# A decode kernel's gate moved ahead of six query rounds, its down product moved to TensorE, two transfers cut in halves

## The chip, the cores and the metric

The kernel runs on one core of a Trainium2 chip. The metric is device time in microseconds (us). Of the kernel before, three runs took 696.61, 697.62 and 699.97 us; the median is 697.62. One more execution was recorded by the hardware profiler.

The engines have short names in the profile: PE is TensorE (PEld its weight loads), DVE is VectorE, ACT is ScalarE, POOL is GpSimd, SP is SyncE, which issues nearly all transfers here. "Queue" means SP's transfer queue. A "handover" is one engine's wait for another's semaphore.

## The reference

One token of a decoder block. `x` is one row of 512, normed to `xn`. Attention has 32 heads of 128 against cached keys and values of 8192 positions; a gated unit of 1376 columns gives a row of 512, whose silu scales the attention's output.

```
xn = layernorm(x)
q  = (xn @ wq).reshape(32 heads, 128)
p  = softmax(q . k_cache * 128**-0.5)          # 8192 positions a head
s  = (p @ v_cache).reshape(4096) @ wo          # 4096 -> 512
h  = sigmoid(xn @ w_gate) * (xn @ w_up)        # 1376
g  = silu(h @ w_down)                          # 512
out = x + s * g
```

All in float32. Keys and values are 134 MB each, so 268 of the 294 MB that the kernel reads.

## The kernel before, in words

Heads are taken in 16 pairs. The keys of a pair are one transfer of 8.39 MB into a slot of 128 partitions by 16384 numbers (64 partitions a head, 128 positions on each); its values are another. SBUF has room for three such slots, A, B and C. The keys of pairs 0, 2, 4, ... go to B and those of odd pairs to A; the values of all pairs but the last go to C, those of the last to B. K0 is the keys of pair 0, V0 its values, and so on.

**Transfers.** SP issues them in program order, and each waits until its slot is free: `wq` into C, the three weights of the gated unit into A, K0 into B (L144 to L151). Then K1 into A, once the gate is done (L322, L323: a wait on `n_gate`, the count after the matmuls of L258). Then V0 into C, once all eight rounds of queries have read `wq` (L332: a wait on `s_q`), and from there by turns K(n+2), which waits for VectorE to be done with the keys of pair n (`k_free`, L338), and V(n+1), which waits for PE to be done with the values of pair n (`s_po`, L335). At the end come V15 into B (L341) and `wo` into C in five pieces (L344).

**Queries** (L210 to L222). A round t makes 512 columns of `xn @ wq`, four heads, with four matmuls into PSUM bank t. The moving operand is `wq`, the stationary one is `xn` spread over 128 columns (`xnb`). ACT copies each round into `q_all`. Rounds 0 to 3 run first (L226), rounds 4 to 7 behind the turned products of the gated unit (L241).

**Gated unit.** VectorE makes the weighted sums of `w_gate` and `w_up` over four blocks of rows (L198, L201), and PE sums these over the partitions and turns them, 11 matmuls of one column each (L235, L236), into banks 0 and 1. Sigmoid (L240) and a product (L244) give `hid`. VectorE then multiplies the ten full blocks of `w_down` by their columns of `hid` and adds them up (L247: L198, L201) and the last block of 96 rows (L250). PE sums over the partitions with four matmuls (L258), ACT takes the sigmoid (L262), and VectorE multiplies it by its argument after the scores of pair 0 (L330).

**A pair.** VectorE multiplies the keys by the query and sums over 128 numbers, in two halves (L277, L279: four passes), then takes the maximum (L282), which PE turns and spreads (L304, L306). ACT takes the exponentials into `prz` (L293). PE adds up the row sums (L308), multiplies `prz` with the values in 32 matmuls in four column groups (L313), and picks the heads' rows (L318). On PE pairs 0 to 14 are a loop (L347), pair 15 stands behind it (L349).

**End.** The heads are divided by their sums and turned (L356 to L364), multiplied by `wo` (L374, L378: a wait for each piece), scaled by the gate, and added to `x` (L391, L393).

Each engine follows its own program in order; nothing reorders it.

Of the kernel before, what the change touches and what calls it, by code (L numbers as in the profile page):

```python
# [25 lines left out]
def kernel(  # L26
# [17 lines left out]
    NP = H // 2  # L44
# [62 lines left out]
    po, pt, pm, g_ps, acc, fold_ps, o_ps, oTl = bank  # L107

# [7 lines left out]
    names = "x xr wg wu wd wr wq k0 k1 va".split()  # L116
# [34 lines left out]
    d["k0"].by(sp.dma_start(B, rows_of(k_src, 0)), 16)  # L151
# [12 lines left out]
    dve.memset(rs2, 0.0)  # L164
    dve.wait_ge(s_pool.sem, 2)
# [60 lines left out]
    queries(0, nq // 2)  # L226
# [3 lines left out]
    for a, (name, t) in enumerate((("wg", wg_t), ("wu", wu_t))):  # L230
# [7 lines left out]
        if a == 0:  # L238
            act.wait_ge(s_pe.sem, n)
            n_sg = s_act.by(act.activation(sg, turned[0], AF.Sigmoid))  # L240
    queries(nq // 2, nq)  # L241
    dve.wait_ge(s_act.sem, n_sg)
    dve.wait_ge(s_pe.sem, n)
    s_dve.by(dve.tensor_mul(hid, sg, turned[1]))  # L244
    self_wait()
    dve.wait_ge(d["wd"].sem, 16)
    weighted(wd_t[:, 0, :], lambda r: wd_t[:, r, :], lambda r: hid[:, r:r + 1], FP)  # L247
    self_wait()
    dve.wait_ge(d["wr"].sem, 16)
    s_dve.by(dve.scalar_tensor_tensor(wd_t[:FL, 0, :], wd_rest[:FL, :], hid[:FL, FP:FP + 1], wd_t[:FL, 0, :],  # L250
                                      op0=ALU.mult, op1=ALU.add))
    n_wr = s_dve.n
    pool.wait_ge(s_dve.sem, n_wr)
    n_prz = s_pool.by(pool.memset(prz.rearrange("p j a -> p (j a)"), 0.0))
    act.wait_ge(s_pool.sem, n_prz)
    pe.wait_ge(s_dve.sem, n_wr)
    for g in range(NG):
        m = pe.matmul(g_ps[g * GP:g * GP + 1, :GC], ones[:, 0:1], wd_t[:, 0, g * GC:(g + 1) * GC],  # L258
                      start=True, stop=True)
# [9 lines left out]
    def scores(n):  # L269
        kt = k_slot(n).rearrange("p (j d) -> p j d", d=Dh)  # L270
        s = sc[n % 2]
        h = NB // 2
        q = q_all[:, n:n + 1, :].to_broadcast([P, h, Dh])
        dve.wait_ge(k_sem(n).sem, 16 * (n // 2 + 1))
        for i in range(2):
            part = kt[:, i * h:(i + 1) * h, :]
            s_dve.by(dve.tensor_mul(part, part, q))  # L277
# [24 lines left out]
    def pair(v, landed):  # L302
# [3 lines left out]
        pe.matmul(pm[:, 0:2], ones[:1, :], mx[:1, 2:4], start=True, stop=True).then_inc(s_pm, 1)  # L306
        take(pe, s_pr)
        pe.matmul(oTl[:, 2:4], ones, rs2, start=True, stop=True)  # L308
        nj = NB // ROWS
        landed()  # L310
        for j in range(nj):
            g = j % NG
            m = pe.matmul(po[g * GP:g * GP + 2 * ROWS, :], prz[:, j * ROWS:(j + 1) * ROWS, :],  # L313
                          v[:, j * QT:(j + 1) * QT], start=(j < NG), stop=(j >= nj - NG))
# [26 lines left out]
    d["va"].by(sp.dma_start(B, rows_of(v_src, NP - 1)), 16)  # L341
# [87 lines left out]
```

## Time and profile before

| | |
|---|---|
| profiled execution, its own time | 697.02 us |
| its span in the trace | 695.1 us |
| DVE busy | 587.8 us (85%) |
| PE busy | 241.8 us (35%) |
| ACT busy | 41.4 us (6%) |
| SP's queue | 97.8% of 16 engines' span |
| read from HBM | 293.67 MB |
| mean TensorE clock granted | 0.651 |

Rows of groups read: line, engine, operation, out<-in, shapes, count, then busy time and idle time ahead of it. Rows in order of time read: start, duration, engine, line, operation, and in brackets the idle time before it with what ended it. Rows by stretch read: stretch, its length, then PE, PEld, DVE, ACT and POOL busy time (with counts of instructions), granted TensorE clock, DMA share, GB/s. One float32 matmul is two instructions in these rows.

### The profile page before, as it was taken

What the parts mean: (1) busy time and instruction counts of PE and PEld (TensorE: products, weight loads), DVE (VectorE), ACT (ScalarE), POOL (GpSimd) and SP (SyncE); (2) the same over time, 40 slices, a digit from 0 to 9 for tenths busy, and PEclk for the clock granted to TensorE, in tenths of its full rate; (3) what the DMA queues carried; (4) which work ended last, traced back from release to release, by engine and by line L of the source; (5) the groups of instructions that cost most, each with busy time, mean ns of one, the idle gap of its engine ahead of it and who ended that gap; (6) DMA issues with size and microseconds to landing.
All of it is one profiled execution on the core that took longest, in us unless ns stands there. A gap on an engine that the chain in (4) does not pass through costs nothing. (4 is left out here: it accounts for less than half of the span.)

```text
span 695.1 us, 3534 instructions
## 1 busy us (share of the span) xinstructions
PE 241.8 (35%) x1490; PEld 91.0 (13%) x1490; DVE 587.8 (85%) x140; ACT 41.4 (6%) x135; POOL 1.0 (0%) x7
## 2 busy tenths in 40 slices
PE   0499005123060505043140506051230605050367
PEld 0274001101010101001010101011010101010022
DVE  0348999999989989798979989798979899798950
ACT  0021010101010000001010000001010100000010
POOL 0000000000000000000000000000000000000000
PEclk9988556657565757556575756565575656575579
DMA  9994999999999999999999999999999999999997
GB/s 392 402 465 192 420 422 422 426 457 441 427 422 426 434 456 434 422 426 426 460 437 422 426 422 464 437 422 426 422 464 434 426 426 422 464 434 426 426 420 307
DMA packets 6181, 293.74 MB, mean 423 GB/s; under 512 B 824, under 2 KB 832, under 8 KB 1184
## 3 DMA queue, kind: packets, MB, share of 16 engines
q1 hardware_dynamic: 5912, 293.47, 97.8%
q10 hardware_dynamic: 264, 0.20, 0.1%
q8 instruction: 3, 0.05, 0.0%
q14 instruction: 2, 0.02, 0.0%
HBM read 293.67 MB, written 0.00 MB: 422 GB/s over the span
## 5 line engine op out<-in xcount | busy, mean ns | idle before, releaser
L277 DVE TENSOR_TENSOR slot<-slot,q_all 128x8192 f32<-128x8192 f32 x32 | 277.9, 8684 | 31.2 <-DMA slot<-in_A_k_cache_dram 31.2
L279 DVE TENSOR_REDUCE sc<-slot 128x64 f32<-128x8192 f32 x32 | 277.9, 8686 | 1.1
L313 PE MATMUL psum<-slot,prz 128*8 128x512 f32 x1024 | 146.9, 738 | 272.2 <-PEq L130 272.2
L313 PEld LDWEIGHTS psum<-slot,prz 128*8 128x8 f32 x1024 | 30.1, 103 | 375.5 <-issue 375.4
L304 PE MATMUL psum<-ident,mx 128*1 128x128 f32 x32 | 9.4, 395 | 107.3 <-PEq L130 107.3
L297 ACT COPY o<-psum 128x512 f32<-128x512 f32 x16 | 9.4, 585 | 431.5 <-PE psum L313 431.5
L213 PE MATMUL psum<-slot,o 128*128 x64 | 32.7, 676 | 1.6 <-DVE o L204 1.6
L318 PE MATMUL psum<-pick,o 128*128 128x2 f32 x128 | 16.4, 250 | 12.8 <-PEq L130 12.8
L318 PEld LDWEIGHTS psum<-pick,o 128*128 128x128 f32 x128 | 15.5, 191 | 27.2 <-issue 27.2
L308 PE MATMUL psum<-rs,ones 128*128 128x2 f32 x32 | 8.9, 349 | 23.4 <-PEq L130 23.4
L179 DVE TENSOR_REDUCE st<-x_col 128x1 f32<-128x4 f32 x1 | 0.2, 157 | 19.9 <-DMA x_col<-in_A_x_dram 19.9
L213 PEld LDWEIGHTS psum<-slot,o 128*128 128x128 f32 x64 | 13.8, 220 | 19.0 <-issue 19.0
L304 PEld LDWEIGHTS psum<-ident,mx 128*1 128x1 f32 x32 | 1.8, 80 | 108.4 <-issue 108.4
L284 DVE TENSOR_REDUCE mx<-psum 1x2 f32<-1x128 f32 x16 | 4.5, 279 | 12.3 <-PE psum L304 12.3
L293 ACT ACTIVATE prz<-sc,mx 64x128 f32<-64x128 f32 x32 | 13.0, 405 | 0.7
L356 DVE RECIPROCAL heads<-heads 128x32 f32<-128x32 f32 x1 | 0.4, 354 | 13.4 <-ACT heads L299 13.4
L306 PE MATMUL psum<-mx,ones 1*128 1x2 f32 x32 | 8.9, 344 | 7.4 <-PEq L130 7.4
L308 PEld LDWEIGHTS psum<-rs,ones 128*128 128x128 f32 x32 | 8.0, 312 | 24.3 <-issue 24.3
L289 ACT ACTIVATE mx<-psum 128x2 f32<-128x2 f32 x16 | 2.8, 172 | 129.8 <-PE psum L306 129.8
L201 DVE SCALAR_TENSOR_TENSOR slot<-slot,xn 128x1376 f32<-128x1376 f32 x6 | 9.9, 1652 | 0.2
L306 PEld LDWEIGHTS psum<-mx,ones 1*128 1x128 f32 x32 | 8.0, 307 | 14.9 <-issue 14.9
L175 PE MATMUL psum<-st,ones 128*128 128x1 f32 x4 | 1.2, 362 | 24.8 <-DVE st L179 23.9
(57 smaller groups left out, 72.5 us busy)
## 6 DMA issues: line engine op xcount, KB each, us to landing
slot<-in_A_wo_dram SPq DMA_DIRECT2D x1, 4096.0 KB, 19.1
slot<-in_B_w_gate_dram SPq DMA_DIRECT2D x1, 2752.0 KB, 28.2
slot<-in_B_w_up_dram SPq DMA_DIRECT2D x1, 2752.0 KB, 34.2
slot<-in_B_w_down_dram SPq DMA_DIRECT2D x1, 2560.0 KB, 39.7
slot<-in_A_wo_dram SPq DMA_DIRECT2D x1, 2048.0 KB, 23.5
slot<-in_A_wo_dram SPq DMA_DIRECT2D x1, 1280.0 KB, 26.1
slot<-in_A_wo_dram SPq DMA_DIRECT2D x1, 512.0 KB, 26.9
slot<-in_A_k_cache_dram SPq DMA_DIRECT2D x16, 42.4
```

The costliest lines, as they stand in the source:

```text
L201: s_dve.by(dve.scalar_tensor_tensor(acc, t(k), col(k), acc, op0=ALU.mult, op1=ALU.add))
L213: m = pe.matmul(psum[:, bass.ds(t * QT, QT)], xnb[:, k, :], wq_t[:, k, bass.ds(t * QT, QT)], start=(k == 0), stop=(k == KT - 1))
L277: s_dve.by(dve.tensor_mul(part, part, q))
L279: s_dve.by(dve.reduce_sum(s[:, i * h:(i + 1) * h], part, axis=AX.X))
L284: dve.reduce_max(mx[:1, 2:4], pt[:1, :P].rearrange("p (a m) -> p a m", a=2), axis=AX.X).then_inc(s_am, 1)
L293: e = act.activation(prz[r, :, a], sc[n % 2][r, :], AF.Exp, bias=mx[r, 4 + a:5 + a], scale=SCALE, accum_out=rs2[r, a:a + 1])
L297: act.copy(o1, po).then_inc(s_o1, 1)
L304: pe.matmul(pt[:1, :P], mx[:, 0:1], ident, start=True, stop=True).then_inc(s_pt, 1)
L306: pe.matmul(pm[:, 0:2], ones[:1, :], mx[:1, 2:4], start=True, stop=True).then_inc(s_pm, 1)
L308: pe.matmul(oTl[:, 2:4], ones, rs2, start=True, stop=True)
L313: m = pe.matmul(po[g * GP:g * GP + 2 * ROWS, :], prz[:, j * ROWS:(j + 1) * ROWS, :], v[:, j * QT:(j + 1) * QT], start=(j < NG), stop=(j >= ...
L318: m = pe.matmul(oTl[:, 0:2], o1[:, b * Dh:(b + 1) * Dh], pick[:, 2 * b:2 * b + 2], start=(b == 0), stop=(b == ROWS - 1))
```

## The change

It has four parts. Line numbers behind the first part are 1 to 16 higher in the changed kernel.

1. Only query rounds 0 and 1 run ahead of the gated unit. Rounds 2 to 7 follow once the gate's row is finished (`n_grow`). The down product is no longer VectorE's: PE takes `hid` as stationary column and the blocks of `w_down` as moving operand, in four column groups of one bank (`gate_ps`), VectorE copies the bank (`gsum`), and four matmuls with `sel`, a column of ones at the four groups' rows, add the groups up. Sigmoid and product follow at once. VectorE clears the two banks at the program's start. The clearing of `prz` moves from GpSimd to VectorE.
2. K0 comes in two transfers of half the columns each, and the scores of pair 0 begin on the first half.
3. V15 comes in two such transfers, and its product begins on the first half.
4. In pair 15 PE runs four matmuls of 512 columns into `g_ps`, whose result nobody reads: three ahead of the maximum, one ahead of the row sums.

```diff
-    queries(0, nq // 2)
+    queries(0, 2)
...
-    queries(nq // 2, nq)
     dve.wait_ge(s_act.sem, n_sg)
     dve.wait_ge(s_pe.sem, n)
-    s_dve.by(dve.tensor_mul(hid, sg, turned[1]))
-    self_wait()
-    dve.wait_ge(d["wd"].sem, 16)
-    weighted(wd_t[:, 0, :], lambda r: wd_t[:, r, :], lambda r: hid[:, r:r + 1], FP)
...
+    n_hid = s_dve.by(dve.tensor_mul(hid, sg, turned[1]))
+    pe.wait_ge(s_dve.sem, n_hid)
+    pe.wait_ge(d["wd"].sem, 16)
+    for r in range(FP):
+        g = r % NG
+        m = pe.matmul(gate_ps[g * GP:g * GP + 1, :], hid[:, r:r + 1], wd_t[:, r, :], start=(r < NG), stop=(r >= FP - NG + 1))
+    pe.wait_ge(d["wr"].sem, 16)
+    g = FP % NG
+    m = pe.matmul(gate_ps[g * GP:g * GP + 1, :], hid[:FL, FP:FP + 1], wd_rest[:FL, :], start=False, stop=True)
+    n_gate = s_pe.by(m)
+    dve.wait_ge(s_pe.sem, n_gate)
+    n = s_dve.by(dve.tensor_copy(gsum, gate_ps))
+    pe.wait_ge(s_dve.sem, n)
     for g in range(NG):
-        m = pe.matmul(g_ps[g * GP:g * GP + 1, :GC], ones[:, 0:1], wd_t[:, 0, g * GC:(g + 1) * GC],
-                      start=True, stop=True)
-    n_gate = s_pe.by(m)
-    act.wait_ge(s_pe.sem, n_gate)
-    n_gs = s_act.by(act.activation(g_row, g_ps[:, :GC], AF.Sigmoid))
+        m = pe.matmul(g_ps[g * GP:g * GP + 1, :GC], sel, gsum[:, g * GC:(g + 1) * GC], start=True, stop=True)
+    n = s_pe.by(m)
+    act.wait_ge(s_pe.sem, n)
+    n = s_act.by(act.activation(g_row, g_ps[:, :GC], AF.Sigmoid))
+    dve.wait_ge(s_act.sem, n)
+    n_grow = s_dve.by(dve.tensor_mul(g_row, g_row, g_ps[:, :GC]))
+    n_prz = s_dve.by(dve.memset(prz.rearrange("p j a -> p (j a)"), 0.0))
+    pe.wait_ge(s_dve.sem, n_grow)
+    act.wait_ge(s_dve.sem, n_prz)
+    queries(2, nq)
...
-    d["k0"].by(sp.dma_start(B, rows_of(k_src, 0)), 16)
+    for name, c in (("ka", slice(0, SLOT // 2)), ("k0", slice(SLOT // 2, SLOT))):
+        d[name].by(sp.dma_start(B[:, c], rows_of(k_src, 0)[:, c]), 16)
...
+    def busy(count):
+        for _ in range(count):
+            pe.matmul(g_ps, ones, q_all[:, :QT // Dh, :], start=True, stop=True)
...
-    pair(B, lambda: pe.wait_ge(d["va"].sem, 16))
+    pair(B, {0: lambda: pe.wait_ge(d["va"].sem, 16), NB // ROWS // 2: lambda: pe.wait_ge(d["vb"].sem, 16)}, (3, 1))
```

The program of PE around the gate, before. Slot_55 is A, slot_56 is B, slot_57 is C, o_59 is `xnb`; a row within the loop of L211 stands once and runs for each round:

```order
L213 MATMUL psum<-slot_57,o_59 128x512
L211 REGISTER_ALU
L211 COMPARE_AND_BRANCH
L235 MATMUL psum<-ones,slot_55 128x1 [waits s_dve,s_act]
L235 MATMUL psum<-ones,slot_55 128x1 x9
L236 MATMUL psum<-ones,slot_55 96x1
...
L211 UNCONDITIONAL_BRANCH
L211 ISA
L213 MATMUL psum<-slot_57,o_59 128x512
...
L258 MATMUL psum<-slot_55,ones 1x128 [waits s_dve]
L258 MATMUL psum<-slot_55,ones 1x128 x3
```

And now (L217 is the query matmul, L239 the turned products, L252 and L255 the down product, L261 its groups' sum):

```order
L217 MATMUL psum<-slot_57,o_59 128x512
L215 REGISTER_ALU
L215 COMPARE_AND_BRANCH
L239 MATMUL psum<-ones,slot_55 128x1 [waits s_dve,s_act]
...
L252 MATMUL psum<-slot_55,hid 1x512 [waits d_wd,s_dve]
L252 MATMUL psum<-slot_55,hid 1x512 x9
L255 MATMUL psum<-wd_rest,hid 1x512 [waits d_wr]
L261 MATMUL psum<-wd_rest,pick 1x128 [waits s_dve]
L261 MATMUL psum<-wd_rest,pick 1x128 x3
L215 UNCONDITIONAL_BRANCH [waits s_dve]
L215 ISA
```

The second loop of queries, now six rounds, stands behind the gate and waits for VectorE (`n_grow`); the down product has come to PE, ahead of it.

VectorE between the second weighted sum and the scores of pair 0, before:

```order
L244 TENSOR_TENSOR hid<-sg,psum 128x11 [waits s_pe,s_act]
L198 TENSOR_SCALAR slot_55<-slot_55,hid 128x512 [waits d_wd,s_dve]
L201 SCALAR_TENSOR_TENSOR slot_55<-slot_55,hid 128x512 [waits s_dve] x9
L250 SCALAR_TENSOR_TENSOR slot_55<-wd_rest,hid,slot_55 96x512 [waits d_wr,s_dve]
L277 TENSOR_TENSOR slot_56<-slot_56,q_all 128x8192 [waits d_k0,s_act]
```

And now:

```order
L247 TENSOR_TENSOR hid<-sg,psum 128x11 [waits s_pe,s_act]
L258 COPY wd_rest<-psum 128x512 [waits s_pe]
L266 TENSOR_TENSOR g_row<-g_row,psum 128x128 [waits s_act]
L267 MEMSET prz 128x256
L288 TENSOR_TENSOR slot_56<-slot_56,q_all 128x8192 [waits d_ka,s_act]
```

Eleven sums are gone, three short steps have come in, each behind another engine, and the scores wait for the first half of K0 only.

SP's first issues behind `w_down`, now:

```order
L153 DMA slot_56<-in_A_k_cache_dram 128x8192 x2
L274 DMA slot_55<-in_A_k_cache_dram 128x16384 [waits s_pe]
L351 DMA slot_57<-in_A_v_cache_dram 128x16384 [waits s_q]
L274 DMA slot_56<-in_A_k_cache_dram 128x16384 [waits s_dve]
L351 DMA slot_57<-in_A_v_cache_dram 128x16384 [waits s_po]
```

But for K0's two halves this is the order of before; what has moved is the place on PE at which `s_pe` and `s_q` reach the counts that K1 and V0 wait for.

More of the change, by code (lines that the diff above doesn't have):

```diff
@@ L107 @@
     po, pt, pm, g_ps, acc, fold_ps, o_ps, oTl = bank
+    gate_ps, gsum = fold_ps, wd_rest
     sems = []
@@ L114, in semaphore @@
         return sems[-1]
-    names = "x xr wg wu wd wr wq k0 k1 va".split()
+    names = "x xr wg wu wd wr wq ka k0 k1 va vb".split()
     d = {n: Count(semaphore(f"d_{n}")) for n in names}
@@ L164 @@
     dve.memset(rs2, 0.0)
+    dve.memset(gate_ps, 0.0)
+    dve.memset(g_ps[:, :GC], 0.0)
     dve.wait_ge(s_pool.sem, 2)
@@ L240 @@
             n_sg = s_act.by(act.activation(sg, turned[0], AF.Sigmoid))
-    queries(nq // 2, nq)
     dve.wait_ge(s_act.sem, n_sg)
     dve.wait_ge(s_pe.sem, n)
-    s_dve.by(dve.tensor_mul(hid, sg, turned[1]))
-    self_wait()
-    dve.wait_ge(d["wd"].sem, 16)
-    weighted(wd_t[:, 0, :], lambda r: wd_t[:, r, :], lambda r: hid[:, r:r + 1], FP)
[L248 to L256, printed above, removed]
-    for g in range(NG):
-        m = pe.matmul(g_ps[g * GP:g * GP + 1, :GC], ones[:, 0:1], wd_t[:, 0, g * GC:(g + 1) * GC],
-                      start=True, stop=True)
-    n_gate = s_pe.by(m)
-    act.wait_ge(s_pe.sem, n_gate)
-    n_gs = s_act.by(act.activation(g_row, g_ps[:, :GC], AF.Sigmoid))
+    n_hid = s_dve.by(dve.tensor_mul(hid, sg, turned[1]))
[11 more added lines that the diff above has]
+    pe.wait_ge(s_dve.sem, n)
+    for g in range(NG):
+        m = pe.matmul(g_ps[g * GP:g * GP + 1, :GC], sel, gsum[:, g * GC:(g + 1) * GC], start=True, stop=True)
[8 more added lines that the diff above has]
+    queries(2, nq)
     def load_k(n):
@@ L273, in scores @@
         q = q_all[:, n:n + 1, :].to_broadcast([P, h, Dh])
-        dve.wait_ge(k_sem(n).sem, 16 * (n // 2 + 1))
+        if n == 0:
+            dve.wait_ge(d["ka"].sem, 16)
         for i in range(2):
+            if i == (n == 0):
+                dve.wait_ge(k_sem(n).sem, 16 * (n // 2 + 1))
             part = kt[:, i * h:(i + 1) * h, :]
@@ L299, in softmax, with pair @@
         s_act.by(act.copy(heads[:, n, :], oTl[:, 0:4]))
-    def pair(v, landed):
+    def busy(count):
+        for _ in range(count):
+            pe.matmul(g_ps, ones, q_all[:, :QT // Dh, :], start=True, stop=True)
+    def pair(v, waits, keep=(0, 0)):
+        busy(keep[0])
         take(pe, s_rm)
@@ L306, in pair @@
         pe.matmul(pm[:, 0:2], ones[:1, :], mx[:1, 2:4], start=True, stop=True).then_inc(s_pm, 1)
+        busy(keep[1])
         take(pe, s_pr)
@@ L309, in pair @@
         nj = NB // ROWS
-        landed()
         for j in range(nj):
+            if j in waits:
+                waits[j]()
             g = j % NG
@@ L327 @@
         scores(n)
-        if n == 0:
-            dve.wait_ge(s_act.sem, n_gs)
-            s_dve.by(dve.tensor_mul(g_row, g_row, g_ps[:, :GC]))
         softmax(n)
@@ L340 @@
     sp.wait_ge(s_dve.sem, k_free[NP - 2])
-    d["va"].by(sp.dma_start(B, rows_of(v_src, NP - 1)), 16)
+    for name, c in (("va", slice(0, SLOT // 2)), ("vb", slice(SLOT // 2, SLOT))):
+        d[name].by(sp.dma_start(B[:, c], rows_of(v_src, NP - 1)[:, c]), 16)
     sp.wait_ge(s_po, NP - 1)
@@ L347 @@
     with nc.Fori(0, NP - 1, engines=[pe.engine], head_slot={pe.engine: 0}):
-        pair(C, lambda: take(pe, d_v, 16))
-    pair(B, lambda: pe.wait_ge(d["va"].sem, 16))
+        pair(C, {0: lambda: take(pe, d_v, 16)})
+    pair(B, {0: lambda: pe.wait_ge(d["va"].sem, 16), NB // ROWS // 2: lambda: pe.wait_ge(d["vb"].sem, 16)}, (3, 1))
     turn = A[:, :P]
```

## The prediction

> **What bounds the kernel now.** I read the page's slices first, then busy time by stretch, then SyncE's waits and issues, then the first 100 us in order of time. The page's slices (40 of 17.4 us) show the transfers full throughout but for one place:
>
> ```profile
> DMA  9994999999999999999999999999999999999997
> GB/s 392 402 465 192 420 422 422 426 457 441 427 422 426 434 456 434 422 426 426 460 437 422 426 422 464 437 422 426 422 464 434 426 426 422 464 434 426 426 420 307
> ```
>
> That is the mark of a kernel bound by its transfers: VectorE idles a little in each pair, the DMA engines never, except in the fourth slice (192 GB/s). Busy time by stretch (the last two columns are DMA share and GB/s) puts the hole at 60 to 70.5 us, with 433 GB/s from there to 690:
>
> ```profile
> 60.00:70.50 10.50, 9.85 (x31) 4.01 (x29) 9.54 (x3) 2.38 (x8) 0.31 (x1) 1.00 0.00 0
> 70.50:690.00 619.50, 195.73 (x1298) 64.86 (x1298) 556.48 (x102) 31.80 (x114) 0.00 (x0) 0.62 1.00 433
> ```
>
> SyncE's waits name the cause: the second key transfer (K1, L266) waits for the matmuls of L258, the end of the gate.
>
> ```profile
> SPq L266 <- PE psum L258: 65.7, 1, 65.7
> ```
>
> How long the hole is, I take from landings, since the share by stretch books packets whole (5.59 of 1 in a quarter of a microsecond, below). Four looks at single issues, K0, K1, V0 and V14, each with its start and its time to landing:
>
> ```profile
> L151 SPq DMA_DIRECT2D slot<-in_A_k_cache_dram x1: 497/497/497, 3.7 to 3.7; - x1
> DMA to landing us min/median/max: 58.5/58.5/58.5
> ...
> L266 SPq DMA_DIRECT2D slot<-in_A_k_cache_dram x1: 328/328/328, 69.9 to 69.9; - x1
> DMA to landing us min/median/max: 23.2/23.2/23.2
> ...
> L336 SPq DMA_DIRECT2D slot<-in_A_v_cache_dram x1: 432/432/432, 70.3 to 70.3; - x1
> DMA to landing us min/median/max: 42.2/42.2/42.2
> ...
> L336 SPq DMA_DIRECT2D slot<-in_A_v_cache_dram x1: 328/328/328, 623.6 to 623.6; - x1
> DMA to landing us min/median/max: 29.7/29.7/29.7
> ```
>
> K0 lands at 62.2, K1 at 93.1, V0 at 112.5, V14 at 653.3. From V0 to V14 lie 28 transfers of 8.39 MB (K2 to K15, V1 to V14): 540.8 / 28 = 19.3 us each. K0 to K1 takes 30.9, so the hole costs 30.9 - 19.3 = **11.6 us**. An issue into an empty queue lands 23.2 us later, 3.9 more than the queue's own pace; so a transfer costs nothing if it is issued 3.9 us or more before the one ahead of it lands, and at best a little later: after K1's issue at 69.9 the first packets start in this stretch, 0.85 us on.
>
> ```profile
> 70.75:71.00 0.25, 0.00 (x0) 0.00 (x0) 0.25 (x1) 0.00 (x0) 0.00 (x0) 1.00 5.59 1835
> ```
>
> The start in order of time, with the rows that made the gate late:
>
> ```profile
> 27.62 15.78 PE L213 MATMUL psum<-slot,o 128*128 x32 [1.62 <-DVE o L204]
> ...
> 36.57 0.74 ACT L221 COPY q_all<-psum 64x256 f32<-64x256 f32 x2 [2.69 <-PE psum L213]
> ...
> 37.89 5.03 DVE L201 SCALAR_TENSOR_TENSOR slot<-slot,xn 128x1376 f32<-128x1376 f32 x3
> ...
> 42.81 4.81 PEld L235 LDWEIGHTS psum<-ones,slot 128*128 128x128 f32 x20 [0.24 <-issue]
> ...
> 47.91 0.18 ACT L240 ACTIVATE sg<-psum 128x11 f32<-128x11 f32 x1 [2.43 <-PE psum L236]
> ...
> 52.58 16.94 PE L213 MATMUL psum<-slot,o 128*128 x32
> ...
> 52.83 0.17 DVE L244 TENSOR_TENSOR hid<-sg,psum 128x11 f32<-128x11 f32 x1 [9.92 <-PE psum L236]
> ...
> 53.56 7.05 DVE L201 SCALAR_TENSOR_TENSOR slot<-slot,hid 128x512 f32<-128x512 f32 x9
> ...
> 60.64 0.75 DVE L250 SCALAR_TENSOR_TENSOR slot<-wd_rest,hid,slot 96x512 f32<-96x512 f32 x1
> ...
> 62.32 8.69 DVE L277 TENSOR_TENSOR slot<-slot,q_all 128x8192 f32<-128x8192 f32 x1 [0.93 <-DMA slot<-in_A_k_cache_dram]
> ...
> 69.45 0.40 PE L258 MATMUL psum<-slot,ones 128*1 128x128 f32 x8
> ...
> 98.54 8.67 DVE L277 TENSOR_TENSOR slot<-slot,q_all 128x8192 f32<-128x8192 f32 x1
> ```
>
> VectorE has the down product ready at 61.4, but the four matmuls of L258 stand in PE's queue behind rounds 4 to 7 of the queries (52.58 to 69.5). So K1 waits for query rounds that it does not need.
>
> **The change, part by part: the gate ahead of six rounds.** A matmul here is two instructions. TensorE runs at two speeds, seen in the time from one query weight load to the next (its own time and the idle time before it):
>
> ```profile
> 54.43 0.34 PEld L213 LDWEIGHTS psum<-slot,o 128*128 128x128 f32 x1 [0.52 <-issue]
> ...
> 59.49 0.19 PEld L213 LDWEIGHTS psum<-slot,o 128*128 128x128 f32 x1 [0.24 <-issue]
> ...
> 56.00:58.00 2.00, 2.00 (x4) 0.83 (x3) 1.93 (x3) 0.00 (x0) 0.00 (x0) 0.50 1.21 524
> 58.00:60.00 2.00, 2.00 (x6) 0.83 (x5) 1.89 (x4) 0.73 (x2) 0.00 (x0) 0.86 1.21 524
> ```
>
> 0.86 us an instruction at a granted clock of 0.50, 0.43 at full, with the change at 58.5, 6 us after the run began; the run at 27.62 got there in 3.6 us (its first eight matmuls, two rounds, take until 36.57, where the copy starts).
>
> Now the new order. Rounds 0 and 1 end at 36.5, as before. The turned products of L235 need their banks copied out (36.57 + 0.74 = 37.3) and the gate's weighted sum; they take from 42.81 to 47.91, 5.1 us: now 37.4 to 42.5. Those for the up weights wait for VectorE's up sum (37.89 + 5.03 = 42.9): 43.0 to 48.0. `hid` takes 0.2, and at 48.4 the down product can start on PE; its weights are there, as the page's table of issues tells (issued between 2.3 and 3.7, 39.7 to landing):
>
> ```profile
> slot<-in_B_w_down_dram SPq DMA_DIRECT2D x1, 2560.0 KB, 39.7
> ```
>
> It is 11 matmuls of 512 columns with one output row each, in four column groups: 22 instructions. The nearest rows are the output product's, of the same shape, in the tail:
>
> ```profile
> 685.17 5.33 PE L374 MATMUL psum<-slot,o_all 128*1 128x512 f32 x48 [0.28 <-DVE o_all L364]
> ...
> 690.46 0.98 PEld L378 LDWEIGHTS psum<-slot,o_all 128*1 128x1 f32 x40 [0.90 <-DMA slot<-in_A_wo_dram]
> ...
> 692.27 0.11 PEld L378 LDWEIGHTS psum<-slot,o_all 128*1 128x1 f32 x8 [0.17 <-DMA slot<-in_A_wo_dram]
> ...
> L341 SPq DMA_DIRECT2D slot<-in_A_v_cache_dram x1: 327/327/327, 630.2 to 630.2; - x1
> DMA to landing us min/median/max: 42.4/42.4/42.4
> ...
> 672.68 8.86 PE L313 MATMUL psum<-slot,prz 128*8 128x512 f32 x64
> ```
>
> 48 in 5.33 us at full clock, so 2.4 us for 22, or 4.9 at half; I take half and 0.2 of latency, since the one-column products of L235 before it had brought the clock down: **gate product done at 53.5** (51 at best). K1 is issued there, 8.7 us before K0 lands; 3.9 are needed. **The hole of 11.6 us closes**, with 4.8 us to spare.
>
> **What is late next: V0.** SyncE then waits for all eight rounds (`s_q`) before it may load V0 over the query weights, and nothing else is in its queue until then but K2, behind it. K1 now lands at 62.2 + 19.3 = 81.5, so V0 is free if issued by 77.6 (by 3.9 us ahead), perhaps by 80.6 (0.85 us). Six rounds start when the gate row is done: a PSUM copy on VectorE (0.75, as L250), four small matmuls (0.40 to 0.6), sigmoid and multiply on 128 columns (I estimate 0.3 each, between L240's 0.18 on 11 columns and L250's 0.75 on 512), and the handovers between them: 53.5 + 2.4 = 55.9. 24 matmuls are 48 instructions: 20.6 us at full clock, end 76.5; a cold start of 3.6 to 6 us costs half of that, 1.8 to 3.0, end 79.5. Middle 78.2. Loss against 77.6: 0.6, bounds 0 (warm, or the later limit) and 1.9 (79.5). **I take +0.6.** ACT's copies of rounds 2 and later (0.74 a round) are first needed by pair 4, so their delay costs nothing.
>
> [...]
>
> [...]
>
> **First keys in halves; VectorE's relief.** The eleven sums of L198, L201 and L250 go (about 8.3 us, 53.04 to 61.4). With K0's first half landing about 9.7 us before the second, scores of pair 0 start behind the gate row and prz's memset, at about 56.1 instead of 62.32. Slot B is then free at 56.1 + 4 x 8.69 = 90.9, where K2's issue came at:
>
> ```profile
> 97.08 0.33 SPq L266 DMA_DIRECT2D slot<-in_A_k_cache_dram  x1
> ```
>
> K2 must be issued by 100.8 - 3.9 = 96.9 once V0 lands at 100.8. So the halves gain nothing by themselves, but without them K2 would stand at the limit (97.1). The two new PSUM memsets (each below L250's 0.75) lie where VectorE waits for x, and prz's memset delays the scores alone, with 6.0 us to spare. Zero; if the halves' lead were all lost, 97.1 - 96.9 = 0.2.
>
> **Tail: values in halves, four spare matmuls.** V15 lands at 672.6 and its product starts at 672.68 behind row sums: no wait to take away, at most 0.1. The spare matmuls (0.86 each warm, 1.7 cold) may let the last pair run warm: 8.86 to 64 instructions / 4 x 0.43 = 6.9, a gain of 2.0; run cold, the one between the maximum's broadcast and the row sums may hold up the chain by 1.7, while the three lie under VectorE's last pass (8.69). Either way the end is set by the last output weights: L378 waits twice for them, 0.90 and 0.17 us, and they are the queue's last transfer. So a gain of 2.0 is hidden, and a loss shows for at most 1.7 - 0.9 = 0.8. Zero.
>
> **Sum**, against the profiled execution (697.0, span 695.1): -11.6 + 0.6 = -11.0, so 686.0. The median of the runs (697.6) is 0.6 above it: **686.6 us**.
>
> **Rivals**, times on the median's scale. *The clock stays low longer*, 12 us at half instead of 6: six rounds end at 55.9 + 20.6 + 6 = 82.5, V0 is 4.9 late, 690.9. For it: PE has 0.50 for most of the program. Against: both query runs here were at full speed within 6 us.
>
> *Slower: the gate comes late.* If it is g us late, K1 is late by g - 4.8 and V0 against K1 by 0.6 + 4.8, together g + 0.6: each microsecond costs one, and beyond g = 11.0 the change loses. If the 22 instructions did not overlap in the column groups they would take 22 x 0.86 = 18.9, g = 13.8: 697.6 - 11.6 + 14.4 = 700.4. Against it: L374's 48 in 5.33 us.
>
> *Each extra transfer costs a fixed price.* The output weights, five transfers, end 19.7 us after V15's landing (672.6 to 692.27) against 19.3 for one: 0.1 each, so two more cost 0.2. If instead each paid all that an issue into an empty queue pays, 3.9, it would be 7.8: 694.4. Against it: those five transfers. [...]
>
> *The gain does not reach the end*: the transfers start earlier and something else, VectorE or a buffer, holds them by the same amount: 697.6. Against it: VectorE needs 36.2 us a pair (62.32 to 98.54), the queue 38.6.
>
> **How the numbers follow.** Forecast 0.83; low clock 0.08; late gate 0.03; fixed price 0.03; no gain 0.03. What can be told from no change is 0.5%, 3.5 us: faster 0.94, same 0.03, slower 0.03. The forecast's own range goes from 685.0 (no loss at V0, and 1.0 below, as the lowest run before lies 1.0 under its median) to 689.3 (1.9 lost at V0, 0.8 in the tail, 0.6 of scatter); stretched by 0.6 below, and above to most of the low clock's case, it is 684.4 to 690.5.
>
> **What would show it.** Right: no zero stretch near 60 to 70 us, K1's landing 19.3 us after K0's, its issue near 53.5; V0 issued near 78 and landing 19.3 to 21 us after K1; K2 issued near 91; L378's counterpart still waiting for output weights. Wrong: SyncE's longest wait of the start on the query rounds, with a new hole near 80 us; the gate product taking over 10 us; landings over 20 us apart later on.

## The result and the profile after

The changed kernel takes **687.18 us** in the median (686.87 to 688.25, 6 runs), the one before in the same session 698.71 us (696.61 to 700.86, 6 runs). The ratio is **0.9837, with a 95% interval of 0.9814 to 0.9861**: 11.5 us, or 1.6%, faster. The forecast was 686.6 within 684.4 to 690.5. The profiled execution after took 687.08 us with a span of 685.2, against 697.02 and 695.1 before: 9.9 us of span. Two executions of the kernel before in later sessions, at 716.2 and 970.8 us, lie far outside the others and stand in no ratio below.

The page's slices (40 of 17.1 us) of the changed kernel, DMA busy in tenths and GB/s:

```profile
DMA  8999999999999999999999999999999999999996
GB/s 371 417 440 428 437 460 440 425 432 433 428 428 432 432 428 436 463 428 432 432 432 428 428 432 432 428 444 455 432 432 428 432 428 428 432 432 436 428 437 292
```

The slice of 192 GB/s is gone. Busy time by stretch of 60 to 70.5 us, which held 0 GB/s before (the last two columns are DMA share and GB/s):

```profile
60.00:70.50 10.50, 10.50 (x26) 4.63 (x25) 10.47 (x2) 2.20 (x6) 0.00 (x0) 1.00 1.04 449
```

SyncE's waits (us in total, times, longest), of the changed kernel. K1 (L274) now waits for the gate's product and V0 (L351) for the last query round:

```profile
SPq L274 <- PE psum L255: 48.5, 1, 48.5
...
SPq L351 <- PE psum L217: 24.3, 1, 24.3
```

The start in order of time (start, duration, engine, line; in brackets the idle time before):

```profile
48.70 4.07 PE L252 MATMUL psum<-slot,hid 128*1 128x512 f32 x18 [0.34 <-DVE hid L247]
...
53.26 0.33 SPq L274 DMA_DIRECT2D slot<-in_A_k_cache_dram  x1
...
55.27 8.63 DVE L288 TENSOR_TENSOR slot<-slot,q_all 128x8192 f32<-128x8192 f32 x1
...
55.33 22.56 PE L217 MATMUL psum<-slot,o 128*128 x48 [0.92 <-DVE g_row L266]
...
58.58 0.33 PEld L217 LDWEIGHTS psum<-slot,o 128*128 128x128 f32 x1 [0.52 <-issue]
59.27 0.19 PEld L217 LDWEIGHTS psum<-slot,o 128*128 128x128 f32 x1 [0.36 <-issue]
...
77.92 0.33 SPq L351 DMA_DIRECT2D slot<-in_A_v_cache_dram  x1
```

The gate's product runs at half clock (0.50 until 52.3 us) for nearly all its length, and K1 is issued at 53.26, 16.6 us earlier than before. The clock granted is full between 52.5 and 55.5 us and half again from 56 to 59: it falls as the six query rounds begin at 55.33. They take 0.85 us an instruction until 59.3, then 0.43, and end at 77.9, where V0 is issued. And the landings, from the rows of single issues (K0's two halves, K1, V0, and V14):

```profile
L153 SPq DMA_DIRECT2D slot<-in_A_k_cache_dram x2: 463/472/482, 3.8 to 4.3; - x2
DMA to landing us min/median/max: 49.2/53.8/58.3
...
L274 SPq DMA_DIRECT2D slot<-in_A_k_cache_dram x1: 328/328/328, 53.3 to 53.3; - x1
DMA to landing us min/median/max: 28.7/28.7/28.7
...
L351 SPq DMA_DIRECT2D slot<-in_A_v_cache_dram x1: 328/328/328, 77.9 to 77.9; - x1
DMA to landing us min/median/max: 24.7/24.7/24.7
...
L351 SPq DMA_DIRECT2D slot<-in_A_v_cache_dram x1: 327/327/327, 613.9 to 613.9; - x1
DMA to landing us min/median/max: 29.6/29.6/29.6
```

K0 is whole at 4.27 + 58.3 = 62.6, K1 lands at 82.0, V0 at 102.6, V14 at 643.5. From V0 to V14, 28 transfers take 540.8 us, 19.3 each, as before. V0 landed at 112.5 before: the 9.9 us of the span are all there by V0's landing, and nothing behind it gives any back. One gap is odd: K0 to K1 19.4, but K1 to V0 20.7.

The tail of the changed kernel:

```profile
660.67 2.08 PE L315 MATMUL psum<-q_all,ones 128*128 128x512 f32 x2
...
662.54 0.43 PE L325 MATMUL psum<-rs,ones 128*128 128x2 f32 x2
...
662.89 8.90 PE L331 MATMUL psum<-slot,prz 128*8 128x512 f32 x64
...
675.43 5.33 PE L390 MATMUL psum<-slot,o_all 128*1 128x512 f32 x48 [0.28 <-DVE o_all L380]
680.58 1.28 PE L394 MATMUL psum<-slot,o_all 128*1 128x128 f32 x40
```

The first three spare matmuls ran warm (2.82 us at 653.59), but the clock fell again before the fourth (0.50 from 660 to 662 us), which took 2.08 us. Pair 15's product is no warmer than before (8.90 against 8.86), the output product as warm (5.33). Behind it the weight loads of L394 still wait 0.58 us for the last output weights.

### The profile page after: what moved, and what is told of

The parts are those of the page before. It is cut to its first block, busy times and chain, and to the rows that moved or that the text cites. A ratio compares the mean times of both kernels' runs of the same rounds, so it can differ in the third digit from the quotient of the medians.

```text
span 685.2 us, 3587 instructions
## 1 busy us (share of the span) xinstructions
PE 249.6 (36%) x1520; PEld 93.2 (14%) x1520; DVE 581.2 (85%) x133; ACT 41.4 (6%) x135; POOL 0.7 (0%) x6
## 5 line engine op out<-in xcount | busy, mean ns | idle before, releaser
L217 PE MATMUL psum<-slot,o 128*128 x64 | 31.6, 656 | 2.5 <-DVE o L208 1.6
L217 PEld LDWEIGHTS psum<-slot,o 128*128 128x128 f32 x64 | 13.3, 211 | 19.5 <-issue 19.5
L325 PEld LDWEIGHTS psum<-rs,ones 128*128 128x128 f32 x32 | 8.1, 311 | 23.9 <-issue 23.9
## 6 DMA issues: line engine op xcount, KB each, us to landing
slot<-in_A_k_cache_dram SPq DMA_DIRECT2D x2, 4096.0 KB, 53.8
```

The costliest lines, as they stand in the source:

```text
L217: m = pe.matmul(psum[:, bass.ds(t * QT, QT)], xnb[:, k, :], wq_t[:, k, bass.ds(t * QT, QT)], start=(k == 0), stop=(k == KT - 1))
```

## The experiments

The theory: the gain is the hole in SyncE's queue and comes from the order on PE. The rivals: it comes from the moved product alone; or from the halves and the spare matmuls. Three questions were open beside it: whether V0's late issue costs the 1.3 us seen above, where a late gate or a late V0 begins to cost, and what the spare matmuls are worth. Line numbers differ by a few from kernel to kernel. All kernels compute the whole output; what some add is work whose result nobody reads. They ran in three sessions, in which the kernel before took 700.2, 699.7 and 697.1 us in the median; a ratio is always to the kernel before of the same session. The first section below is the first session; no_halves, tail_warm and after_again are the third; the others are the second.

### The parts one by one

**gate_only**: the change without halves and spare matmuls.

```diff
-    for name, c in (("ka", slice(0, SLOT // 2)), ("k0", slice(SLOT // 2, SLOT))):
-        d[name].by(sp.dma_start(B[:, c], rows_of(k_src, 0)[:, c]), 16)
+    d["k0"].by(sp.dma_start(B, rows_of(k_src, 0)), 16)
...
-    pair(B, {0: lambda: pe.wait_ge(d["va"].sem, 16), NB // ROWS // 2: lambda: pe.wait_ge(d["vb"].sem, 16)}, (3, 1))
+    pair(B, {0: lambda: pe.wait_ge(d["va"].sem, 16)})
```

> The changed kernel with K0 and V15 whole again and without the four spare matmuls: the gate part of the change alone. Theory (the whole gain is the closed hole in SP's queue): 687 to 688, ratio 0.983 to 0.986. The scores of pair 0 start at 62.3 again instead of 55.3, K2 is issued near 97 instead of 90, which is 5 us ahead of V0's landing and costs 0 to 0.5 us. Rival (VectorE's earlier start on pair 0, or the halves and the spare matmuls, carry part of the gain): 690 or more, with transfers over 19.5 us apart behind V0.

Measured: 688.93 us (686.49 to 690.64), ratio 0.9841 (0.9799 to 0.9884). As far as four runs can tell, the whole gain is there, and V0 lands at 102.2, as in the change. K2, which without K0's halves is issued at 98.46, 3.8 us ahead of V0's landing, still lands 19.5 us after V0.

**order_only**: the kernel before, with rounds 2 to 7 put behind the gate's row, which is finished at once for that. The down product stays on VectorE.

```diff
-    queries(0, nq // 2)
+    queries(0, 2)
...
-    queries(nq // 2, nq)
...
     n_gs = s_act.by(act.activation(g_row, g_ps[:, :GC], AF.Sigmoid))
+    dve.wait_ge(s_act.sem, n_gs)
+    n_grow = s_dve.by(dve.tensor_mul(g_row, g_row, g_ps[:, :GC]))
+    pe.wait_ge(s_dve.sem, n_grow)
+    queries(2, nq)
```

> The kernel before with rounds 2 to 7 of the queries moved behind the gate, the down product still on VectorE, transfers whole. Theory (order is what counts, the product's engine only sets how late the gate is): VectorE's sums end near 57.2, K1 is issued near 57.8, in time within 0.5 us; the query rounds start 3.3 us later than in the changed kernel and colder, V0 is issued near 82 and lands 23 to 24.5 us after K1. 689.5 to 691, ratio about 0.988. Rival (the gain comes from taking 8 us of work off VectorE): 696 to 698.

**product_only**: the product on PE as in the change, but rounds 4 to 7 ahead of it, as before; K0 and V15 whole, no spare matmuls. (The lines are against the changed kernel.)

```diff
-    queries(0, 2)
+    queries(0, nq // 2)
...
+    queries(nq // 2, nq)
     dve.wait_ge(s_act.sem, n_sg)
...
-    queries(2, nq)
```

> The changed kernel's down product on TensorE, but left behind query rounds 4 to 7 as the gate was before; four rounds ahead, transfers whole, no spare matmuls. Theory: the gate is done near 72, K1 is issued 2 us later than before and lands 33 us after K0: 699 to 701 against 698, ratio 1.003. The scores of pair 0 wait for the gate here and start near 73; K2 is then issued near 108, still ahead of V0's landing. Rival (VectorE's relief gives the gain): below 694.

Measured: order_only 694.11 us (692.63 to 695.0), ratio 0.9925 (0.9901 to 0.995); product_only 700.78 us (698.02 to 702.71), ratio 1.0016 (0.9996 to 1.0035). In order of time, order_only's end of the gate and its first two issues:

```profile
57.71 0.60 PE L258 MATMUL psum<-slot,ones 128*1 128x128 f32 x8 [8.73 <-DVE slot L250]
...
58.38 0.33 SPq L270 DMA_DIRECT2D slot<-in_A_k_cache_dram  x1
...
83.01 0.33 SPq L337 DMA_DIRECT2D slot<-in_A_v_cache_dram  x1
```

With VectorE's product K1 comes at 58.38, still in time (it lands 19.3 us after K0), but the queries end at 83.0 and V0 is issued 0.8 us after K1's landing; it lands 23.9 us after K1. Order without product closes the hole at K1 and opens a smaller one at V0, which lands at 106.1 instead of gate_only's 102.2. The landing came as expected, 6.4 us ahead of before, and the median is 6.1 us below that of its session. Its 694.1 us is 3 to 4.5 us above what was expected because the expectation went by the 697.6 of before's first three runs, and not by the 700.2 that the kernel before took beside these runs. (The output product of its profiled execution was cold, 8.17 us and not 5.33; what that is worth follows below.) Product without order gets nothing: K1 is issued at 72.21, into the hole of before. So the order alone gives some 6 of the 11 us, the product alone none, and behind the order the product on PE gives the rest, by keeping V0 in time.

**rest_only**: the kernel before with the halves of K0 and V15 and the four spare matmuls, no more.

```diff
-    d["k0"].by(sp.dma_start(B, rows_of(k_src, 0)), 16)
+    for name, c in (("ka", slice(0, SLOT // 2)), ("k0", slice(SLOT // 2, SLOT))):
+        d[name].by(sp.dma_start(B[:, c], rows_of(k_src, 0)[:, c]), 16)
...
-    pair(B, lambda: pe.wait_ge(d["va"].sem, 16))
+    pair(B, {0: lambda: pe.wait_ge(d["va"].sem, 16), NB // ROWS // 2: lambda: pe.wait_ge(d["vb"].sem, 16)}, (3, 1))
```

> The kernel before with K0 and V15 in halves and the four spare matmuls, gate untouched. Theory: none of the three is on the path; ratio 0.999 to 1.001, the hole of 11.6 us stays. [...] Rival (the spare matmuls warm the last pair and the end follows): 696.

Measured: 697.37 us (eight of ten runs 696.6 to 697.6, two at 700.3 and 703.3), ratio 0.9977 (0.9952 to 1.0001). Two transfers more cost nothing: V0 lands at 112.4 and the second half of V15 at 672.6, against 112.5 and 672.6 before. So the rival of a fixed price for each is refuted. The median is 2.9 us below that of before in its session, although the lowest runs are nearly the same (696.6 and 697.0); the ratio, which the two high runs enter, makes it 1.6 us. Why the middle moves and the lowest runs do not is the question of the tail, below.

### What a late V0 costs

**fill**: the change without spare matmuls, query round 2 put between the gate's product and its row, so that the rounds end some 3 us earlier.

```diff
     n = s_dve.by(dve.tensor_copy(gsum, gate_ps))
+    queries(2, 3)
     pe.wait_ge(s_dve.sem, n)
...
-    queries(2, nq)
+    queries(3, nq)
```

(The groups' sum goes to bank 1, and VectorE's multiplication for the gate's row behind the first pass of pair 0.)

> The changed kernel without the spare matmuls and with query round 2 run right behind the down product, in the time in which VectorE copies the bank and ACT makes the sigmoid; the four summing matmuls behind round 2 go to bank 1, and the gate row is finished within the scores of pair 0. PE then pauses no longer between the down product and the queries, and warms earlier. Theory (V0 landed 20.7 instead of 19.3 us after K1 because it was issued only 4.1 us ahead of K1's landing): V0 is issued near 75, 6 to 7 us ahead, lands 19.3 after K1; 1.2 us less than the changed kernel, ratio to it 0.998, about 686. Rival (20.7 has another cause, such as the buffers or the memory's rows): V0 still lands 20.5 or more after K1, no gain.

**v0_late**: eight spare matmuls of 512 columns ahead of rounds 2 to 7. **gate_late**: twenty ahead of the gate's product.

```diff
+    for _ in range(8):
+        pe.matmul(g_ps, ones, o1, start=True, stop=True)
     queries(2, nq)
```

```diff
     pe.wait_ge(d["wd"].sem, 16)
+    for _ in range(20):
+        pe.matmul(g_ps, ones, o1, start=True, stop=True)
```

> The changed kernel with eight spare matmuls of 512 columns between the gate and query round 2: K1 is issued as before near 53.3, V0 about 6.9 us later, near 84.8. Theory (each microsecond by which V0's issue is late costs one): V0 lands 26 to 27.5 us after K1, time 5.4 to 6.9 us longer than the changed kernel, 692.5 to 694. Rival (the later stream makes up for it): within 2 us of the changed kernel.

> The changed kernel with twenty spare matmuls of 512 columns ahead of the down product: the gate is some 18 us late, near 71. Theory (a late gate costs a microsecond for each microsecond, shared between K1 and V0): K1 lands near 94, 31.7 after K0, V0 near 119, 24 to 25 after K1; 16 to 17 us more than the changed kernel, 703 to 705, slower than the kernel before. Rival (only K1's hole counts, V0 is hidden): 698 to 699.

Measured: fill 688.16 us (686.98 to 690.28), ratio 0.9849 (0.9821 to 0.9877); v0_late 690.4 us (689.89 to 690.8), 0.9875 (0.9842 to 0.9908); gate_late 703.9 us (701.74 to 708.16), 1.0084 (1.0053 to 1.0116). v0_late's issue came only 4.2 us later than the change's, not 6.9: the rounds ran at full clock behind the spare matmuls (20.76 us instead of 22.56), and the gate's product was done 0.7 us earlier (K1 at 52.5). Its V0 landed 2.7 us later than the change's, and its median is 3.2 us above; the expected 5.4 to 6.9 went by the later issue. **after_again** is the changed kernel itself, unedited, in another session.

> The changed kernel unaltered, to stand beside the next two on one chip. 687.0 to 688.3 as before. In the runs so far the kernels without spare matmuls fell into two groups, some 3 us apart, by whether the output product (48 instructions) took 5.3 or 8.0 us; theory of the spare matmuls: with them either the last pair's product or the output product is warm in every run, so no run of this one goes above 689.

Measured: 686.95 us (686.8 to 687.93), ratio 0.9843 (0.9818 to 0.9869). The landings of all these kernels, from their first issues ("lead": from V0's issue to K1's landing):

| kernel | K0 whole | K1 issued, landed | V0 issued, landed | lead | K0 to V0 |
|---|---|---|---|---|---|
| after | 62.6 | 53.3, 82.0 | 77.9, 102.6 | 4.0 | 40.1 |
| after_again | 62.3 | 52.5, 83.1 | 75.5, 102.4 | 7.6 | 40.1 |
| fill | 63.6 | 53.4, 83.4 | 74.7, 102.6 | 8.7 | 39.0 |
| gate_only | 63.6 | 53.9, 82.8 | 78.5, 102.2 | 4.2 | 38.6 |
| no_halves (below) | 62.1 | 53.9, 81.4 | 76.9, 102.3 | 4.5 | 40.2 |
| no_spare (below) | 62.5 | 53.8, 81.8 | 78.5, 102.4 | 3.3 | 39.9 |
| v0_late | 63.5 | 52.5, 82.8 | 82.2, 105.3 | 0.7 | 41.8 |
| order_only | 62.9 | 58.4, 82.2 | 83.0, 106.1 | -0.8 | 43.2 |
| gate_late | 63.7 | 70.5, 92.3 | 95.2, 118.2 | -2.9 | 54.5 |
| before | 62.2 | 69.9, 93.1 | 70.3, 112.5 | 22.8 | 50.3 |

With leads from 3.3 to 8.7 us V0 lands at 102.2 to 102.6 all the same. So the change's 20.7 us from K1 to V0 is no late issue: at 7.6 us of lead the same kernel has 19.3 there, and 20.8 between K0 and K1. Later issues do cost; how much can be said once the other cause is known.

What moves by 1.3 to 1.5 us is something else. The changed kernel's DMA queues between 82 and 84 us, and those of after_again between 80 and 82 (packets, MB, share of 16 engines):

```profile
q8 instruction: 1, 0.02, 3.1%
```

```profile
q8 instruction: 1, 0.02, 3.1%
```

That is one 16 KB packet of an instruction queue, about 1 us long (3.1% of 32 us); a second follows at 90 to 92 and 88 to 90. In the changed kernel the first falls just after K1's landing (82.0), in after_again just before it (83.1); the extra time stands in V0 in the one and in K1 in the other. In fill and gate_only a first one falls ahead of K0's landing; there K0 lands at 63.6, in after, after_again, no_halves and no_spare at 62.1 to 62.6, and K0 to V0 is two paces, 38.6 to 39.0. The packet records show how: the 64 KB packets of the keys and values run in sixteen streams, each packet beginning where one ended, 2.42 us apiece. At the first load one stream of the sixteen pauses 0.98 us and its next packet takes 2.89 us, 1.45 in all; at the second load another stream does the same (0.95 and 2.90). Nothing of this is made up for later: from V0 to V14 it is 540.8 us again. The landing of a transfer is that of its last stream: of V0's sixteen in the changed kernel fourteen are in by 101.28 us, the last two, one for each load, at 102.32 and 102.60; of K1's in the kernel before fifteen by 91.87, the last at 93.15. So the first load delays all landings behind it by 1.3 to 1.5 us, and the second, on another stream, adds nothing.

The kernel before has such a load too, at 76.8 us, within K1. Its K1 landed 23.2 us after an issue into the empty queue; so did product_only's (23.0, with a load). gate_late's, into an empty queue with no load between 70 and 92.5 us, took less:

```profile
L276 SPq DMA_DIRECT2D slot<-in_A_k_cache_dram x1: 328/328/328, 70.5 to 70.5; - x1
DMA to landing us min/median/max: 21.8/21.8/21.8
```

So an issue into the empty queue costs 21.8 - 19.3 = 2.5 us, the load 1.3 of its own, and the hole of before without the load was 30.9 - 19.3 - 1.3 = **10.3 us**. The two prices also give the late ones: order_only's V0 should land 0.8 + 21.8 + 1.3 = 23.9 us after K1, which is what it did. Of all issues into the empty queue, gate_late's K1 alone had no load before its landing; the K1 of before, rest_only and product_only and the V0 of order_only, v0_late and gate_late each had one, and each landed 23.0 to 23.2 us after its issue, wherever that stood between 69.9 and 95.2 us. So past the limit each microsecond of delay costs one.

v0_late belongs among them although its lead is 0.7. By its packet records a load at 58.0 us had held one stream back there, K0 landed at 63.5 for it, and K1's landing at 82.8 is that stream's: the last packets of K1 on the other streams had ended by 81.3, so V0's issue at 82.2 found them empty. A lead that is counted against a landing set by one late stream is worth some 1.4 us less. That is why K0 to V0 is 41.8 there and 43.2 in order_only, whose K0 had no load: the two V0s were late alike.

No run removed a load by itself: that they delay the streams is read from the records, not tested by an edit, and what they fetch, and for which engine, stays open: "instruction" is the profile's name for their queue.

gate_late is the rival of the late gate, made real: K1 issued at 70.5, 17.0 us behind the forecast's 53.5, and the kernel 0.8% slower than before. By the prediction's rule for it (each microsecond costs one) it should take 697.6 - 11.6 + 17.0 + 0.6 = 703.6 us; it took 703.9, with runs from 701.7 to 708.2. That the two agree to 0.3 us is luck: the kernel before of its session took 699.7 and not 697.6. The landings bear the rule out better: V0 was expected near 119 and landed at 118.2.

### What the tail is worth

**no_spare**: the change without the four spare matmuls. **no_halves**: the change with K0 and V15 whole, the spare matmuls kept. **tail_warm**: the change with seven spare matmuls ahead of the row sums (6 and 1) and two more in pair 15, ahead of the picks and behind them. The edits in this order (K0 whole in no_halves as in gate_only):

```diff
-    pair(B, {0: lambda: pe.wait_ge(d["va"].sem, 16), NB // ROWS // 2: lambda: pe.wait_ge(d["vb"].sem, 16)}, (3, 1))
+    pair(B, {0: lambda: pe.wait_ge(d["va"].sem, 16), NB // ROWS // 2: lambda: pe.wait_ge(d["vb"].sem, 16)})
```

```diff
-    pair(B, {0: lambda: pe.wait_ge(d["va"].sem, 16), NB // ROWS // 2: lambda: pe.wait_ge(d["vb"].sem, 16)}, (3, 1))
+    pair(B, {0: lambda: pe.wait_ge(d["va"].sem, 16)}, (3, 1))
```

```diff
-    pair(B, {0: lambda: pe.wait_ge(d["va"].sem, 16), NB // ROWS // 2: lambda: pe.wait_ge(d["vb"].sem, 16)}, (3, 1))
+    pair(B, {0: lambda: pe.wait_ge(d["va"].sem, 16), NB // ROWS // 2: lambda: pe.wait_ge(d["vb"].sem, 16)}, (6, 1, 1, 1))
...
+        busy(keep[2])
         take(pe, s_o1)
...
         m.then_inc(s_ot, 1)
+        busy(keep[3])
```

> The changed kernel without the four spare matmuls. Theory: in the changed kernel the fourth of them ran cold for 2.1 us and held up the row sums of pair 15 by 0.45 us, and the product of pair 15 took 8.9 us as before; without them the chain behind pair 15 is 0.45 us earlier and waits for the output weights instead: the time is the same within 0.4 us. Rival (they keep the clock up and gain 2 us): 2 us longer.

> The changed kernel with K0 and V15 whole again, the four spare matmuls kept. Theory (the halves give nothing, only the gate's place and the spare matmuls count): the same as the changed kernel within 0.6 us, 687 to 688.5, K2 issued near 97 to 99 instead of 90 and still landing 19.3 to 19.6 us after V0. Rival (the halves keep K2 in time): 1 to 2 us longer, K2 21 us after V0.

> The changed kernel with six instead of three spare matmuls ahead of pair 15's maximum, and one more on each side of the last pair's picking of rows, so that PE has work from pair 14 to the output product. Theory (the tail's time hangs on TensorE's clock, and the last landing of output weights is the floor): the output product takes 5.3 us in every run, the chain ends within 0.6 us of the last landing, 686.5 to 687.5 with a spread under 1 us; not below, as the changed kernel's profiled run already ended 0.6 us after the last landing. Rival (more spare work delays the chain): 688 or more.

Measured: no_spare 690.0 us, in two groups (687.1, 687.2 and 689.9 to 690.5), ratio 0.9852 (0.9822 to 0.9881); no_halves 688.16 us, 686.9 to 690.7, ratio 0.9851 (0.9824 to 0.9878); tail_warm 687.08 us, 686.92 to 687.09, ratio 0.9841 (0.9816 to 0.9865). The kernel before falls into the same two groups in the first session: of 20 runs, 5 lie at 697.0 to 698.2 and 15 at 699.8 to 701.2. In the two later sessions some of its runs lie between them (698.3 to 699.7); of the nine in the last one six lie below 698.4. The tail of no_spare's profiled execution (690.52 us), and what TensorE's clock did there (the third figure from the right is the clock):

```profile
676.11 7.99 PE L390 MATMUL psum<-slot,o_all 128*1 128x512 f32 x48 [0.28 <-DVE o_all L380]
```

```profile
672.00:674.00 2.00, 1.19 (x12) 0.97 (x8) 0.00 (x0) 0.59 (x1) 0.00 (x0) 1.00 1.03 442
674.00:676.00 2.00, 0.72 (x3) 0.50 (x2) 0.89 (x4) 0.16 (x1) 0.00 (x0) 0.67 0.95 407
676.00:678.00 2.00, 1.89 (x12) 0.40 (x16) 0.05 (x1) 0.00 (x0) 0.00 (x0) 0.50 1.01 431
...
682.00:684.00 2.00, 2.00 (x24) 0.45 (x20) 0.00 (x0) 0.00 (x0) 0.00 (x0) 1.00 0.00 0
```

And the same stretches of the changed kernel:

```profile
672.00:674.00 2.00, 1.02 (x8) 0.97 (x8) 0.14 (x1) 0.62 (x2) 0.00 (x0) 1.00 1.07 459
674.00:676.00 2.00, 0.98 (x10) 0.51 (x14) 0.81 (x4) 0.00 (x0) 0.00 (x0) 1.00 0.95 407
676.00:678.00 2.00, 2.00 (x24) 0.41 (x16) 0.00 (x0) 0.00 (x0) 0.00 (x0) 1.00 0.98 415
```

Between pair 15's product and the output product PE has only the picks and the turning to do. PE is about as busy there in both kernels; in the one the clock falls at about 675 and the output product takes 7.99 us, in the other it holds and the product takes 5.33. The transfers of no_spare are over by 682 us (0 GB/s in the last row), and PE works on alone. The two output products differ by 2.7 us. Pair 15's product was colder too, 0.7 us longer than in the change:

```profile
662.62 9.63 PE L331 MATMUL psum<-slot,prz 128*8 128x512 f32 x64
```

Together they make the 3.4 us by which this execution took longer than the change's (690.52 against 687.08), about the distance between the groups. (Of before only an execution of the lower group was profiled, so that its upper group ends with a cold product is argued from no_spare, not shown.) The clock records of the traces show where the clock changes: in before and in the changed kernel every whole stretch at one clock lasts a multiple of 3.41 us (1 to 13 times), and the instants of change, from the span's start, lie 1.07 us behind such a multiple in the first execution of the changed kernel, 3.27 in after_again, the same kernel, and 2.27 in no_spare. So the same kernel meets these changes at other points of its program in another execution, and the two groups of one and the same kernel agree with that; that this decides between them was not shown.

So the spare matmuls buy no faster best run but fewer slow ones: after and after_again have none above 688.3 in 11, no_spare four of six above 689.8, fill and gate_only, which have none either, two of six and two of four. The profiled executions show how. With the four spare matmuls and V15 in halves, one of the last two products is quick each time: pair 15's takes 8.75 to 8.90 us and the output product 5.33 (after, after_again), or 7.05 to 7.84 and 7.0 (rest_only, v0_late, gate_late). Without spare matmuls both are slow in four of six: 9.41 to 10.0 and 7.88 to 8.17 (no_spare, gate_only, order_only, product_only; in before and fill 8.86 and 9.15, and 5.33). One profile of each kernel makes this a pattern and not a rate. The halves of V15 may do a little of it too. In no_halves the whole V15 makes its product wait, and it ran cold, as the output product did behind it (8.13):

```profile
662.44 9.91 PE L327 MATMUL psum<-slot,prz 128*8 128x512 f32 x64 [0.38 <-DMA slot<-in_A_v_cache_dram]
```

Two of its five runs, 689.0 and 690.7, lie above all of after's; five runs are few for a rate. tail_warm shows where this ends:

```profile
662.27 7.05 PE L331 MATMUL psum<-slot,prz 128*8 128x512 f32 x64
...
672.97 3.61 PE L392 MATMUL psum<-slot,o_all 128*1 128x512 f32 x32 [0.28 <-DVE o_all L382]
...
677.44 1.90 PE L392 MATMUL psum<-slot,o_all 128*1 128x512 f32 x16 [0.86 <-DMA slot<-in_A_wo_dram]
...
680.46 1.27 PE L396 MATMUL psum<-slot,o_all 128*1 128x128 f32 x40 [1.12 <-DMA slot<-in_A_wo_dram]
```

Everything is warm by its times: pair 15's product, 7.05 us, is 1.85 us shorter than in the change, and the output product, 3.61 and 1.90 us, then waits 0.86 and 1.12 us for output weights: the same 687.1 us, with a spread of 0.17. The last landing is the floor: the lowest run of any version, 686.5 in gate_only, is 0.4 us below tail_warm's lowest.

## Why the prediction was right, and where it was not

**The hole closes: right, and its size 1.3 us too large.** The place (PE's queue, rounds 4 to 7 ahead of the gate) and the step times held: gate product done at 53.3 (forecast 53.5), six rounds from 55.3 (55.9), V0 issued at 77.9 (78.2), K2 at 90.0 (91). gate_only shows the gain without the halves and the spare matmuls, product_only that the moved product without the order gains nothing. The term "-11.6" failed in its size. The prediction took the whole excess of K1's landing as hole; 1.3 us of it is an instruction load, which the changed kernel has too, only in another transfer. The term is -10.3. The load is also why its price of an issue into the empty queue, 3.9, was too high: 2.5 without one.

**V0 late, +0.6: the mechanism did not act.** V0 was issued where forecast, and its landing 20.7 us after K1 fell in the range of 19.3 to 21 us that was to show it right. It was right for a wrong reason: fill and after_again issued V0 3.2 and 2.4 us earlier and it landed at the same time. The limit that the prediction took, 3.9 us ahead, was too strict by that same 1.3; a lead of 3.3 cost nothing. The term is 0. The rule behind it, one microsecond for each past the limit, held in v0_late, order_only and gate_late, by the landings 23.0 to 23.2 us after the issue.

**The cold start of the queries: right in size, by another course.** The six rounds took 22.56 us instead of 20.6 at full clock, 2.0 more, within the forecast's 1.8 to 3.0. But the prediction let PE stay cold through the gate; in fact the clock was full from shortly before the product's end (52.3 to 55.7 us), and at 55.7 it fell again, although PE had worked for 1.7 of these 3.4 us. In after_again, the same kernel, the rounds were warm (full clock from 52 us on, 20.86 us, V0 issued at 75.5). Which of the two comes changes from execution to execution, and neither costs anything here.

**The halves of K0: zero, right.** K2 at 98.5 (gate_only) and 97.0 (no_halves) lands 19.5 and 19.3 us after V0. At most the 0.2 that the prediction held open was lost, in gate_only.

**The tail, zero: mis-sized.** Right was that a warmer last product is hidden behind the last output weights: tail_warm shows it. What failed is the step "Either way the end is set by the last output weights": it priced the tail by the one profiled execution of before, in which L374 happened to be warm (5.33 us) and the transfers were last. Many runs end in the other way, some 3 us later, and no transfer hides that: in no_spare PE works on alone from 682 us. There the spare matmuls have a worth: rest_only's ratio of 0.9977 is 1.6 us, though its interval just reaches 1.0001, and no_spare's median is 2.8 us above that of the change, of another session.

**The sum.** Against the profiled execution: forecast -11.0, measured -9.9, made of +1.3 (hole), -0.6 (V0) and +0.4 (K0 landed at 62.6 instead of 62.2, as much as the arrival of `x`, 24.1 against 23.7). The median was forecast 0.6 above the profiled execution and lies 0.1 above it, since the tail is steadier: 1.1 - 0.5 = 0.6 us, the distance from 686.6 to 687.2. So the errors partly cancel, and that the forecast is only 0.6 us off is in part luck. The medians differ by 11.5 us and not by 9.9 for the same reason: before's lies 1.7 us above its profiled execution (698.71 against 697.02), the change's 0.1.

**The rivals.** The low clock for 12 us did not come. The late gate is real as a mechanism (gate_late) but was not late here. (Its price for columns that do not overlap left out the 0.2 us of latency: g would be 14.0 and the time 700.6.) The fixed price of 3.9 us for each transfer is refuted by rest_only: with two more, V15 landed at 672.6 as before. That the gain does not reach the end is refuted by the landings.

## What to carry to other kernels

Where the queue of transfers is the bound, look first for the slice in which it runs empty and for what stands ahead of the releasing instruction on its engine: moving that ahead was worth 10 us, in part only because the moved product kept the next issue in time, while that product's move was worth nothing on its own. Price a late issue by landings, not by the gap of one transfer alone, and look in the same stretch for small transfers of other queues. Ask of a profiled execution whether it is the usual one: here the kernel before had two kinds of end 3 us apart, and the profile showed one of them.

## What the hardware showed that was not expected

- In the changed kernel a 16 KB instruction load of 1 us, at 83.6 us, held up one of sixteen packet streams by 1.45 us, and the landings behind it kept that delay while the queue stayed full; a second load, at 91.1 us on another stream, added nothing to them. In gate_late, where K0 landed at 63.7 (62.1 to 62.6 with no load ahead of it), no delay was left once the queue had run empty: K1 landed 21.8 us after its issue.
- V0 of no_spare, issued 3.3 us ahead of the landing before it, landed at 102.4 like those with leads up to 8.7; K1 of gate_late, issued into the empty queue, took 2.5 us more than the queue's pace of 19.3. In v0_late K1's landing at 82.8, set by one late stream, hid that the others were empty already: V0, issued at 82.2, landed 23.1 us later, like an issue into the empty queue.
- The same kernel ended in two ways 3 us apart (no_spare: 687.1 and 687.2, or 689.9 to 690.5). In no_spare's profiled execution TensorE's clock fell at about 675 us, in the gap ahead of the output product, which took 7.99 us; in the changed kernel's it held, and the product took 5.33. With four spare matmuls 11 runs lie within 1.5 us, with nine five runs within 0.17.
